# Attention and a gated MLP on one core: four buffers of converted weights, five of outputs, and copies on either engine

## The chip, the core and the metric

The kernel runs on one core of one Trainium2 chip. A core has five engines with queues of their own: PE (TensorE, matmuls), DVE (VectorE), ACT (ScalarE), POOL (GpSimd) and SP (SyncE, which here issues nearly all DMAs). Each executes its queue in order; semaphores tie them together. The metric is the device time of one execution in microseconds (us); less is better.

## What is computed

Attention over 8 batches, 12 heads, 448 positions and 64 channels, with normalised q and k, and then a gated MLP on its output:

```python
q_n, k_n = (rmsnorm(q, g_q), rmsnorm(k, g_k))
scores = scale * np.matmul(q_n, k_n.transpose(0, 1, 3, 2))
scores = scores - np.max(scores, axis=-1, keepdims=True)
attn = np.exp(scores)
attn = attn / (np.sum(attn, axis=-1, keepdims=True) + 1e-09)
x = np.matmul(attn, v)                      # (8, 448, 768) after the heads are joined
...
h = gelu(x @ w_in)                          # 768 -> 1024
u, v = h[..., :512], h[..., 512:]
v_n = (v - mu) / np.sqrt(var + 1e-06) * g_ln
v_s = np.einsum('ts,bsd->btd', w_sg, v_n) + b_sg[None, :, None]
out = x + (u * v_s) @ w_out
```

## The kernel before

**Precision.** Nearly every operand is held as two parts, a high and a low one of 16 bits (or two of fp32r for the last product), so that most products are three matmuls, and most conversions are a copy of the high part and a subtraction for the low one.

**Attention.** A unit is two pairs of heads; there are 24 units, three to a batch, and seven row tiles to a unit. For a row tile the PE writes scores `s` for two halves (12 matmuls of 64x448); the DVE takes the row minimum into `nm` (`jk`, 336 of them in all, 14 to a unit); ACT computes the exponential `ex` with its sums. `ex` is split into two 16-bit parts `ahl`, the high half on ACT, the low half on either engine; SP issues a DMA that transposes `ahl` into `at`. `ahl` lies in a ring of NAH = 3 buffers, so a new one waits until a transpose has left an old one. Then PE multiplies `at` by the parts of v (`vh`, `vl`) into `pv`, in two groups of row tiles a unit (four, then three), and spreads the reciprocal sums over partitions with the `row` matmuls. `row` is copied from PSUM by ACT, `sx` = `pv` times `row` is made by the DVE, and from it `xh` (ACT) and `xl` (POOL) are written to the output tile `x` of the unit. `x` lies in a ring of NX = 6: two batches.

**Preparation of a unit.** q and k are loaded (`qk`), squared (`sqk`), summed (`ss`) and scaled by POOL, split into `hl` and transposed by DMA into `qt`.

**Weights.** They arrive as 64-bit words, which the DVE decodes by integer operations: `dec` for w_in (12 chunks, `wi`), `wr` and `wo_l` for w_out (8 chunks). This is done while the first units run.

**MLP of a batch.** `mv` (the v half, 432 matmuls of 512 columns in all), a cluster of gelus on ACT between two loads of its function table, statistics and normalisation (`vg`, `vh`, `vl`), `mu` (the u half), a second cluster, `ms` (the product with w_sg), two operations and a split on the DVE and ACT (`gh`, `gl`), and `mo`, which adds the residual x and the product with w_out. `ot` copies `mo` from PSUM, and SP sends it out. `mo` reads the unit's `x`, so `x` stays occupied until the batch's MLP ends.

**What sets the order.** The code does not run operations in the order in which it is written. It records them on a tape (`Tape.record`), each with a running count as priority, lowered or raised by an offset: MOFF0 for the first batch's MLP, MOFF for the others', WOFF for the weights, GP for the gelu clusters. How many steps of each stream are recorded per pair of heads is set by SC, SV, WR and M0 to ML; WD is the pair at whose end the weights must all have been recorded, and CUTS says after which steps a group of `pv` may be interrupted. A planner (`Tape.schedule`) then plays a list schedule with costs of its own: an engine takes the ready task of the lowest count, PE prefers to stay in its present tile shape within HYST counts, and a copy that may run on two engines goes to the one that ends it earlier (`Tape.either`, `Tape.best`). The letters HI, EL, RW, OT, VH and so on name the engines allowed for a copy. The planner's order is what the engines execute; all operations are emitted by line 441.

Of the kernel before, what the change touches and what calls it, by code (L numbers as in the profile page):

```python
# [22 lines left out]
ASC = 2.0 ** 14  # L23


MOFF, MOFF0, GP = 300, 100, 350

HI, EL, LO, SQ, QH, QL, RW, XH, OT, GH, VH = "A", "VA", "V", "A", "AV", "G", "A", "A", "A", "A", "A"

UP, UNIT, DEN = 18.714973875118524, 2.0 ** -16, 2.0 ** -41  # L30

WR, M0, M1, MR, ML = 3, 8, 7, 11, 11

I0, WD = 5, 6

VC, UC, CP, MERGE = (2,3), (0,1,2), 'A', False

SC, SV = 7, 4

GRAM = False  # L40

# [1 line left out]

BANKS, MOST = 8, dict(pv=2, mm=4, mme=3, sc=6)
NQK, NVR, RAWB = 2, 2, 3
NAT, NAH, NQT, NVH, HLB, GV = 2, 3, 2, 4, 3, 3
NOT, NX, NEX = 2, 6, 2
DEC, XL, VL, WL = 'V', 'G', 'V', 'V'
RQ, OQ, SQ_, VQ, GLAT, KQ, XQ = 'S', 'S', 'S', 'S', (1100, 4000), 'S', 'S'
EXP_SET = "natural_log_exp_and_others"  # L50
BACC_KW = dict(dynamic_dma_scratch_size=1024)
TILE_KW = dict()

SWITCH, HYST = (133, 92), 160
BIAS = dict(A=0, V=0, G=0)
SLACK = (0, 0)
LONG = 500
WOFF = 0
CUTS = (5,14)
CA = 200  # L60
CV = 70
AG = 85
OVER, PATIENCE = dict(V=130, G=150), 300
START = dict(T=60, A=34, V=33, G=85, S=28, N=0)
AGAIN = dict(T=15, A=15, V=15, G=AG, S=15, N=15)

# [39 lines left out]
class Tape:  # L106
# [140 lines left out]
    def best(self, t, e, now, free, avail, port):  # L247

        mine = now + t.alts[e][1] + BIAS[e] + (max(0, port - now - OVER[e]) if t.alts[e][3] else 0)
        for f, (_, occ, _, _) in t.alts.items():  # L250
            if f != e:
                wait = sum(self.tasks[k].occ for p, k in avail[f] if p < t.prio and not self.tasks[k].alts)
                if max(free[f], now) + wait + occ + BIAS[f] < mine:
                    return False
# [194 lines left out]
def kernel(  # L449
# [256 lines left out]
    def load_qk(u, qs=None):  # L706
        if u >= NI // NG:
            return
        qs = qs or [LD[KQ if u else "S"]]
        b, h0 = u // NU, u % NU * 2 * NG  # L710
        qk = ld.tile([P, 2, 2, C7, D], F32, name="qk", bufs=NQK)
        for x, src in enumerate((q, k)):
            for j in range(NG):
                qs[x % len(qs)].dma_start(
                    out=qk[j * HP:(j + 1) * HP, x].rearrange("p h c d -> p h (c d)"),
                    in_=src[b, h0 + 2 * j:h0 + 2 * j + 2].rearrange("h (p c) d -> p h (c d)", c=C7))
        U[u] = dict(qk=qk)
# [161 lines left out]
    def pv(u, e):  # L879
# [12 lines left out]
        for k_, (j, (v_, o, hx)) in enumerate(steps):  # L892
            for h, (ks, c) in enumerate(hx):
                mm(out=pc[h * HP:(h + 1) * HP, j], lhsT=R[NG * u + j][v_][ks, c], rhs=av[ks, o + c, j, 0:n],
                   start=(k_ == 0), stop=(k_ == len(steps) - 1), skip_group_check=True)
            if k_ in CUTS:
                yield
# [222 lines left out]
    def low(gen, off):  # L1120

        def run():
            while True:
                tape.off = off
                tape.cut()
                try:
                    next(gen)
                except StopIteration:
                    return
                finally:  # L1130
                    tape.off = 0
                    tape.cut()
                yield
        return run()
# [6 lines left out]
    pend = None  # L1141
    wts = low(weights(), WOFF)
    load_qk(0, [SP, A] if EARLY else None)
# [116 lines left out]
```

## Time and profile before

| | us |
|---|---|
| median of three runs | 860.46 |
| lowest, highest | 859.57, 861.25 |
| span of the profiled execution | 856.1 |
| busy in it: PE | 739.2 (86%) |
| ACT | 715.0 (84%) |
| DVE | 664.1 (78%) |
| POOL | 364.9 (43%) |

The span goes from the first to the last instruction of one execution; the time of a run, 860.46 us in the median, also holds what lies around it. The shares of busy time are means over stretches with different limits, so the section with the rows cuts the span into four. All kernel operations carry line 441, so that they are told apart by the names of tiles.

### The profile page before, as it was taken

To read this page: it belongs to the slowest core of one execution; us is meant where nothing else is said; L and a number is where in the kernel's file an instruction comes from. 1 tells how busy PE (TensorE), PEld (TensorE's weight loads), DVE (VectorE), ACT (ScalarE), POOL (GpSimd) and SP (SyncE) were. 2 spreads that over 40 slices of the span, in tenths; PEclk is the share of its full clock that TensorE was granted. 3 is DMA by queue.
4 is the path that set the end of the run, shared out by engine and by line. 5 is a ranking of instruction groups with operands and counts; after the bars stand their busy time and mean duration, and the time that the engine had idled before them with its cause. 6 is when DMAs were issued, how large, how long until landed. Compare 5 with 4: busy or idle time off the path is not lost.

```text
span 856.1 us, 21095 instructions
## 1 busy us (share of the span) xinstructions
PE 739.2 (86%) x7766; PEld 471.9 (55%) x7766; DVE 664.1 (78%) x1658; ACT 715.0 (84%) x1480; POOL 364.9 (43%) x505
## 2 busy tenths in 40 slices
PE   0436768735899999999999999999999999999997
PEld 0223434423485568655855578556755586558557
DVE  6889998899967898878877888879877886484150
ACT  4687889997898999998988898899999998786451
POOL 2544442166635544463565356453463454111000
PEclk9667769986999999999999999999999999999999
DMA  6999999699999979999699989999999699637002
GB/s 172 242 256 211 214 216 177 158 205 210 196 238 214 212 154 192 222 216 198 148 201 234 208 165 225 223 184 180 207 216 211 149 204 184 124 73 156 19 1 74
DMA packets 433943, 155.97 MB, mean 182 GB/s; under 512 B 402544, under 2 KB 427696, under 8 KB 433840
## 3 DMA queue, kind: packets, MB, share of 16 engines
q1 hardware_dynamic: 433840, 154.63, 88.7%
q8 instruction: 61, 1.00, 0.5%
q14 instruction: 42, 0.34, 0.1%
HBM read 43.57 MB, written 11.01 MB: 64 GB/s over the span
## 4 chain that ended last, share of the span: by engine, by line
PE 42%; ACT 23%; DVE 16%; DMA 9%; issue 6%; SPq 2%; POOL 2%; ACTq 0%; DVEq 0%; POOLq 0%
PE pv L441 8%; DMA at<-ahl 6%; ACT ex L441 6%; PE s L441 5%; ACT ahl L441 5%; ACT L441 3%; DVE jk L441 3%; DVE dec L441 2%; DVE wr L441 2%; SPq L441 2%; ACT vg L441 1%; ACT u L441 1%; ACT sqk L441 1%; DVE vl L441 1%; DVE ahl L441 1%
## 5 line engine op out<-in xcount | busy, mean ns | idle before, releaser
L441 DVE TENSOR_SCALAR_CACHE_REDUCE jk<-s 128x448 bf16<-128x448 f32 x336 | 199.2, 615 | 36.9 <-PE s L441 36.4
L441 ACT ACTIVATE ex<-s,nm 128x448 int32<-128x448 f32 x336 | 212.4, 637 | 13.4 <-DVE jk L441 13.1
L441 ACT ACTIVATE ahl<-ex 128x896 f16<-128x896 uint16 x184 | 174.2, 953 | 9.0 <-DMA at<-ahl 8.3
L441 PE MATMUL s<-qt 64*64 64x448 f16 x2016 | 137.9, 375 | 48.6 <-DMA qt<-hl 21.7
L441 PE MATMUL pv<-at,vh 128*64 128x192 f16 (+3 forms) x1536 | 130.6, 271 | 28.1 <-DMA at<-ahl 24.9
L441 PEld LDWEIGHTS <-vh 128*64 128x64 f16 (+2 forms) x1792 | 101.4, 111 | 95.6 <-issue 56.8
L441 DVE TENSOR_SCALAR ahl<-ex 128x896 f16<-128x896 uint16 x152 | 113.6, 748 | 33.9 <-ACT ex L441 26.7
L441 PEld LDWEIGHTS <-qt 64*64 64x64 f16 x2016 | 63.0, 111 | 94.2 <-issue 53.4
L441 POOL TENSOR_TENSOR hl<-qk,hl 128x896 f16<-128x896 f32 (+2 forms) x69 | 93.7, 1364 | 32.7 <-DVE hl L441 8.2
L441 POOL TENSOR_TENSOR xl<-sx,xh 128x512 f16<-128x512 f32 (+1 forms) x48 | 50.5, 1052 | 102.4 <-ACT xh L441 58.8
L441 PEld LDWEIGHTS <-wi 128*128 128x128 f16 x576 | 54.7, 100 | 56.5 <-issue 9.9
L441 POOL TENSOR_TENSOR qk<-qk,ny 128x896 f32<-128x896 f32 x46 | 77.7, 1698 | 15.5 <-DVE ahl L441 6.6
L441 PEld LDWEIGHTS <-xh 128*128 128x128 f16 (+1 forms) x648 | 49.9, 102 | 46.2 <-issue 19.1
L441 PE MATMUL pv<-at,vl 128*64 128x192 f16 (+3 forms) x768 | 72.6, 269 | 0.0
L441 POOL TENSOR_TENSOR qk<-qk,gg 128x896 f32<-128x896 f32 x23 | 48.4, 2102 | 54.6 <-ACT sqk L441 32.6
L441 ACT ACTIVATION_READ_ACCUMULATOR ex<-s,nm 128x1 f32 x336 | 70.4, 210 | 0.0
L441 PEld LDWEIGHTS <-vl 128*64 128x64 f16 (+2 forms) x896 | 55.0, 111 | 15.4 <-DVE vl L441 2.8
L441 POOL TENSOR_SCALAR rx<-sums 128x8 f32<-128x8 f32 (+1 forms) x48 | 19.5, 406 | 98.7 <-ACT ex L441 96.8
L441 DVE TENSOR_REDUCE ss<-sqk 128x14 f32<-128x896 f32 x48 | 51.8, 1081 | 10.5 <-ACT sqk L441 10.4
L441 DVE TENSOR_TENSOR sx<-pv,row 128x512 f32<-128x512 f32 (+1 forms) x48 | 29.7, 619 | 28.4 <-PE pv L441 28.4
L441 ACT ACTIVATE sqk<-qk 128x896 f32<-128x896 f32 x48 | 45.8, 954 | 4.3 <-DMA qk<-in_q_dram 3.0
L441 PEld LDWEIGHTS <-xl 128*128 128x128 f16 (+1 forms) x408 | 36.7, 103 | 22.6 <-POOL xl L441 3.9
(1104 smaller groups left out, 1811.5 us busy)
## 6 DMA issues: line engine op xcount, KB each, us to landing
qk<-in_q_dram SPq DMA_DIRECT2D x48, 224.0 KB, 4.4
qk<-in_k_dram SPq DMA_DIRECT2D x48, 224.0 KB, 4.7
out_dram<-ot SPq DMA_DIRECT2D x56, 192.0 KB, 3.4
raw<-in_moe_w_in_dram SPq DMA_DIRECT2D x12, 512.0 KB, 5.1
vr<-in_v_dram SPq DMA_DIRECT2D x32, 192.0 KB, 3.8
vr<-in_v_dram SPq DMA_DIRECT2D x32, 144.0 KB, 3.9
rawo<-in_moe_w_out_dram SPq DMA_DIRECT2D x8, 384.0 KB, 3.9
at<-ahl SPq DMA_TRANSPOSE x168, 4.5
```

Source lines behind the costliest of these rows:

```text
L441: ins = getattr(q.nc_eng, op)(*first, *a, **kw)
```

## The change

It changes numbers and letters alone; every operation and its operands stay, and only engine, order and buffers differ.

- `ahl` gets four buffers (NAH), `x` five (NX). Both are 3584 bytes per partition.
- `row` (RW), `ot` (OT) and `vh` (VH, the normalised v of the MLP) may be copied by ACT or by the DVE instead of by ACT alone.
- MOFF0, GP, M1, ML, WOFF, WD, SV and CUTS move the recording of the MLP, the gelu clusters, the weights and `pv`.
- HYST, BIAS, OVER and PATIENCE alter the planner's choices.

```diff
--- before.py
+++ after.py
@@ -23,19 +23,19 @@
 ASC = 2.0 ** 14
 
 
-MOFF, MOFF0, GP = 300, 100, 350
-
-HI, EL, LO, SQ, QH, QL, RW, XH, OT, GH, VH = "A", "VA", "V", "A", "AV", "G", "A", "A", "A", "A", "A"
+MOFF, MOFF0, GP = 300, 60, 492
+
+HI, EL, LO, SQ, QH, QL, RW, XH, OT, GH, VH = "A", "VA", "V", "A", "AV", "G", "AV", "A", "VA", "A", "AV"
 
 UP, UNIT, DEN = 18.714973875118524, 2.0 ** -16, 2.0 ** -41
 
-WR, M0, M1, MR, ML = 3, 8, 7, 11, 11
-
-I0, WD = 5, 6
-
-VC, UC, CP, MERGE = (2,3), (0,1,2), 'A', False
-
-SC, SV = 7, 4
+WR, M0, M1, MR, ML = 3, 8, 10, 11, 12
+
+I0, WD = 5, 4
+
+VC, UC, CP, MERGE = (2, 3), (0, 1, 2), "A", False
+
+SC, SV = 7, 3
 
 GRAM = False
 
@@ -43,24 +43,24 @@
 
 BANKS, MOST = 8, dict(pv=2, mm=4, mme=3, sc=6)
 NQK, NVR, RAWB = 2, 2, 3
-NAT, NAH, NQT, NVH, HLB, GV = 2, 3, 2, 4, 3, 3
-NOT, NX, NEX = 2, 6, 2
-DEC, XL, VL, WL = 'V', 'G', 'V', 'V'
+NAT, NAH, NQT, NVH, HLB, GV = 2, 4, 2, 4, 3, 3
+NOT, NX, NEX = 2, 5, 2
+DEC, XL, VL, WL = 'V', "G", "V", 'V'
 RQ, OQ, SQ_, VQ, GLAT, KQ, XQ = 'S', 'S', 'S', 'S', (1100, 4000), 'S', 'S'
 EXP_SET = "natural_log_exp_and_others"
 BACC_KW = dict(dynamic_dma_scratch_size=1024)
 TILE_KW = dict()
 
-SWITCH, HYST = (133, 92), 160
-BIAS = dict(A=0, V=0, G=0)
+SWITCH, HYST = (133, 92), 137
+BIAS = dict(A=0, V=0, G=-200)
 SLACK = (0, 0)
 LONG = 500
-WOFF = 0
-CUTS = (5,14)
+WOFF = -22
+CUTS = (2, 19)
 CA = 200
 CV = 70
 AG = 85
-OVER, PATIENCE = dict(V=130, G=150), 300
+OVER, PATIENCE = dict(V=160, G=150), 351
 START = dict(T=60, A=34, V=33, G=85, S=28, N=0)
 AGAIN = dict(T=15, A=15, V=15, G=AG, S=15, N=15)
```

In the order that the planner makes, ACT gives away 31 of 56 `ot`, 26 of 48 `row` and 21 of 32 `vh`, and takes over 9 `ahl` and 7 `hl`; the DVE has the opposite. PE has the same 7747 matmuls.

The first place is the DVE while it decodes w_out, in the MLP of batch 0 (`wr` and `wo_l` are decoded weights, `jk` the row minima, `mv` and `st` the statistics of the layer norm, `ry` the reciprocal sums). Before:

```order
L441 TENSOR_TENSOR wo_l<-wr,wo_h 128x384
L441 TENSOR_SCALAR jk,nm<-s 128x448
L441 TENSOR_SCALAR wr<-rawo 128x384
L441 TENSOR_SCALAR jk,nm<-s 128x448
L441 TENSOR_SCALAR wr<-wr 128x384
L441 RECIPROCAL ry<-rx 128x6
L441 TENSOR_SCALAR jk,nm<-s 128x448 x2
L441 TENSOR_SCALAR wr<-wr 128x384
L441 TENSOR_SCALAR jk,nm<-s 128x448 x2
L441 SCALAR_TENSOR_TENSOR wr<-rawo,wr 128x384
```

After:

```order
L441 TENSOR_SCALAR wr<-rawo 128x384
L441 BN_AGGR mv<-st 128x2
L441 BN_STATS st<-vg 128x6
L441 TENSOR_SCALAR wr<-wr 128x384
L441 TENSOR_SCALAR wr<-rawo 128x384
L441 TENSOR_SCALAR wr<-wr 128x384 x2
L441 SCALAR_TENSOR_TENSOR wr<-rawo,wr 128x384
L441 TENSOR_SCALAR wr<-wr 128x384
L441 BN_AGGR mv<-st 128x2
```

Steps of the decoding stood singly between row minima; now they stand next to each other beside the statistics of the first layer norm, and the minima come later. The last `wo_l` has 370 instructions ahead of it before, 329 after; there are 78 minima among them before, 59 after.

The second place is ACT where the first output of unit 8 is written (`xh`; `ex` are exponentials, `ahl` converted weights, `sqk` squares, `vh` high parts of v). Before:

```order
L441 ACTIVATE nt_5046<-ss_4884,eps_90 128x28
L441 ACTIVATE ny_5062<-nt_5046 128x28
L441 ACTIVATE xh_5066<-sx_5044 128x4x2x64
L441 ACTIVATE row_5089<-row_5003 128x384
L441 ACTIVATE ex_5114,sums_4882<-s_5048,nm_5098 128x448
L441 ACTIVATE ot_4998<-mo__4947 128x384
L441 ACTIVATE ex_5114,sums_4882<-s_5051,nm_5098 128x448
```

After:

```order
L441 ACTIVATE vh_5160<-vr_4032,v_s_4993 128x448
L441 ACTIVATE xh_5187<-sx_4962 128x4x2x64
L441 ACTIVATE ex_5197,sums_4921<-s_5059,nm_5107 128x448
L441 ACTIVATE vh_5200<-vr_4679,v_s_4993 128x448
L441 ACTIVATE ex_5197,sums_4921<-s_5062,nm_5107 128x448
L441 ACTIVATE ex_5215,sums_4921<-s_5083,nm_5172 128x448
L441 ACTIVATE ahl_5227<-ex_5197 128x896
L441 ACTIVATE xh_5187<-sx_5218 128x3x2x64
L441 ACTIVATE ot_5239<-mo__5146 128x384
```

`xh` of this unit stood behind small steps of the norm, with a `row` copy and `ex` behind it; now it stands behind a copy of v, and exponentials and `ahl` of the next row tile follow it. With five buffers it waits for the last output matmul of batch 1 that reads the tile of unit 3, which on PE stands 195 instructions behind the end of this unit's `pv`; with six the tile of unit 2 was read 1720 instructions before that end.

## Rows read from the trace of the kernel before

**Rows 1.** The page: the span, and the shares of the chain by engine.

```profile
span 856.1 us, 21095 instructions
...
PE 42%; ACT 23%; DVE 16%; DMA 9%; issue 6%; SPq 2%; POOL 2%; ACTq 0%; DVEq 0%; POOLq 0%
```

**Rows 2.** Stretches: length; busy us of PE, PEld, DVE, ACT, POOL; clock, DMA share, GB/s.

```profile
0.00:119.30 119.30, 53.48 (x572) 30.32 (x573) 103.15 (x238) 83.70 (x165) 52.48 (x76) 0.74 1.02 220
119.30:234.90 115.60, 80.26 (x816) 44.67 (x813) 107.04 (x263) 103.56 (x210) 56.29 (x70) 0.86 0.91 190
234.90:780.30 545.40, 534.35 (x5850) 347.67 (x5850) 434.78 (x1115) 496.39 (x1052) 252.06 (x350) 1.00 0.95 190
780.30:856.10 75.80, 71.13 (x532) 49.28 (x530) 19.16 (x47) 31.37 (x56) 4.07 (x10) 0.99 0.22 52
```

**Rows 3.** Timeline of PE: start us, length us, instruction, xcount; two dense places.

```profile
310.53 1.33 PE L441 MATMUL s<-qt 64*64 64x448 f16 x24
311.79 0.44 PE L441 MATMUL pv<-at,vh 128*64 128x192 f16 x6
312.06 0.41 PE L441 MATMUL pv<-at,vl 128*64 128x192 f16 x6
...
272.42 0.59 PE L441 MATMUL mv__3870<-wi,xh 128*128 128x512 f16 x2
272.85 0.38 PE L441 MATMUL mv__3870<-wi,xl 128*128 128x512 f16 x1
```

**Rows 4.** Waits from 235 to 780 us: who waits, for whom, us in total, times, longest.

```profile
DVE ahl L441 <- DMA at<-ahl: 5.2, 6, 2.2
...
ACT ahl L441 <- DMA at<-ahl: 4.3, 6, 1.5
...
PE pv L441 <- DMA at<-ahl: 3.0, 4, 1.5
```

**Rows 5.** Timeline of DVE and PE near the first output matmul of batch 0.

```profile
225.94 0.61 DVE L441 TENSOR_TENSOR gl<-ms__2833,gh 128x448 fp32r<-128x448 f32 x1
...
235.45 0.61 DVE L441 TENSOR_TENSOR gl<-ms__2955,gh 128x448 fp32r<-128x448 f32 x1
...
231.75 0.22 PE L441 MATMUL mo__3068<-idn,xh 128*128 128x128 bf16 x1
```

**Rows 6.** Groups of DVE by form: xcount | busy us, mean ns of one | idle before.

```profile
L441 DVE TENSOR_SCALAR_CACHE_REDUCE jk<-s 128x448 bf16<-128x448 f32 x336 | 199.2, 615 | 36.9 <-PE s L441 36.4
...
L441 DVE DVE_READ_ACCUMULATOR jk<-s 128x1 f32 x336 | 27.5, 82 | 0.0
...
L441 DVE TENSOR_SCALAR ahl<-ex 128x896 f16<-128x896 uint16 x152 | 113.6, 748 | 33.9 <-ACT ex L441 26.7 <-DMA at<-ahl 7.0
...
L441 DVE TENSOR_REDUCE ss<-sqk 128x14 f32<-128x896 f32 x48 | 51.8, 1081 | 10.5 <-ACT sqk L441 10.4
...
L441 DVE CAST hl<-qk 128x896 f16<-128x896 f32 x13 | 12.1, 928 | 1.3 <-POOL qk L441 1.3
...
L441 DVE TENSOR_TENSOR qk<-qk,gg 128x896 f32<-128x896 f32 x1 | 1.1, 1091 | 0.0
...
L441 DVE RECIPROCAL ry<-rx 128x6 f32<-128x6 f32 x24 | 4.5, 187 | 0.9 <-POOL rx L441 0.4
...
L441 DVE TENSOR_TENSOR sx<-pv,row 128x512 f32<-128x512 f32 x24 | 16.5, 687 | 13.6 <-PE pv L441 13.6
...
L441 DVE CAST hl<-qk 128x512 f16<-128x512 f32 x11 | 4.8, 439 | 1.8 <-POOL qk L441 1.8
```

**Rows 7.** Groups of ACT by form, same columns.

```profile
L441 ACT ACTIVATE ahl<-ex 128x896 f16<-128x896 uint16 x184 | 174.2, 953 | 9.0 <-DMA at<-ahl 8.3
...
L441 ACT ACTIVATE row<-row 128x512 f32<-128x512 f32 x24 | 14.4, 602 | 6.0 <-PE row L441 5.9
...
L441 ACT ACTIVATE vh<-vg 128x512 f16<-128x512 f32 x24 | 13.8, 624 | 5.8 <-DVE vg L441 5.8
...
L441 ACT ACTIVATE ot<-mo__4865 128x384 f32<-128x384 f32 x1 | 0.5, 492 | 1.0 <-PE mo__4865 L441 1.0
```


## What was predicted

> **What bounds the kernel now.** I read the span first [rows 1], then the table of four stretches [rows 2], cut where the DVE has finished the 42nd, the 84th and the last of the 336 row minima (`jk`). In the third stretch, 545.4 us long, PE is busy for 534.35 us, or 98%, ACT for 496.39 (91%) and DVE for 434.78 (80%); the granted clock is 1.00, the 2.4 GHz level. In the first two the picture is turned round: between 119.3 and 234.9 us the DVE is busy for 107.04 of 115.60 us, and PE for 80.26. So the program has two halves. Up to about 235 us the DVE decodes the weights and everything queues behind it; afterwards the matmuls queue, almost without holes, until the end.
>
> A busy PE is a weak sign, because the records of pipelined matmuls overlap. So I look at where one starts after another [rows 3]. Twenty-four score matmuls (`s`) take from 310.53 to 311.79 us, 0.0525 us each; six `pv` of 192 columns take from 311.79 to 312.06, 0.045 each; two `mv` of 512 columns take from 272.42 to 272.85, 0.215 each. They follow each other without a pause. In the whole third stretch PE was seen to wait only about 11 us (545.40 less 534.35), of which the wait of `pv` for the transposed weights is 3.0 us [rows 4]. PE's queue is the path there.
>
> The Trainium skill, in "Perfetto Trace Analysis", section "Identifying the Most-Contended Engine", says not to trust matmul busy time, and to take occupancy for ACT and DVE and weight-load time for PE. By that rule ACT (91%) and not PE (weight loads 347.67 of 545.40 us, 64%) is the engine to relieve; what that would give is rival A. The starts one behind another speak against it, so I follow the starts.
>
> **The start of the output phase.** The instants that matter are those at which the first MLP's output matmuls (`mo`, batch 0) can run, since they fill a PE that has otherwise little to do. Before, the first stands at 231.75 us; the second and the fourth `gl` that they need left the DVE at 225.94 and 235.45 [rows 5]. The change records the decoding of the weights earlier (WOFF, WD) and the first MLP at a smaller offset (MOFF0). In the DVE's order the second `gl` is preceded by 388 instructions before the change and 366 after it. What is missing in front of it [rows 6]: 10 `jk` with the reading of their accumulator, 10 x (0.615 + 0.082) = 6.97; 6 `ahl`, 6 x 0.748 = 4.49; 2 `ss`, 2.16; two wide `hl` casts, 1.86; nine shorter ones from `ry` (0.187) to `qk` (1.091), together some 5.0. That is 20.5 us. What is new in front of it: 4 `row` copies and 3 `vh` casts. The trace has neither on the DVE; the nearest rows are `sx` (0.687, also from PSUM) and the `hl` cast of 512 (0.439), so 4 x 0.687 + 3 x 0.439 = 4.1 at most and about 3.6 with the narrow ones. Net: 16.9 us earlier. Up to the fourth `gl` it is 3 `jk`, 2 `ahl` and one `sx` more, 21.1 us. The DVE has hardly a hole there, so the time comes out in full. I take 16.9, since the second `gl` opens the gate, and put the first `mo` at 214.9 us; the other end is 21.1.
>
> This is not all gain, since the postponed attention work has to be made up. By counting the two orders up to the first `mo`, PE has by then issued 432 instead of 504 score matmuls, 384 instead of 480 `pv` (48 fewer of each width), and 128 instead of 156 `row`; the MLP's matmuls are the same 210. Priced from [rows 3]: 72 x 0.0525 = 3.8; 48 x 0.045 = 2.2; 48 wider `pv` at 4/3 of it, 2.9; 28 `row` at 2/3 of it, 0.8. Sum 9.7 us, which PE pays after the first `mo`. From there before needed 856.1 - 231.75 = 624.35 us; the change needs 624.35 + 9.7 = 634.0, and ends at 214.9 + 634.0 = 848.9. That is **-7.2 us**; with the fourth `gl` as gate, -11.4.
>
> **Changes of the matmuls' tile shape.** HYST, CUTS and SV regroup the matmuls on PE. Counted in the order, tile shape changes 365 times before and 351 after; behind the first `mo` it is 289 in both. The 14 saved lie where PE waits anyway. Zero, and at most 14 times some 0.1 us (an estimate from the step between `s` and its neighbours) either way.
>
> **Copies between ACT and DVE.** Counted in the orders, ACT gives the DVE 31 `ot` copies, 26 `row` copies and 21 `vh` casts, and takes back 9 `ahl` and 7 `hl` casts. On ACT that is 31 x 0.492 + 26 x 0.602 + 21 x 0.624 less 9 x 0.953 and less 7 at about the price of `vh` [rows 7], so 44 - 13 = 31 us off at most; on the DVE some 25 to 29 on top, priced as above. In the third stretch the DVE has 545.40 - 434.78 = 110 us free [rows 2], so the addition is covered there; if that cover were gone it would cost its 25 to 29. ACT's relief is worth nothing as long as PE's queue is the path; what is late next is PE itself.
>
> **Four `ahl` buffers.** ACT and DVE waited 4.3 and 5.2 us in the third stretch for a transposing DMA to release one of three buffers [rows 4]. These waits go, but ACT and DVE have slack there. Only the 3.0 us in which `pv` waited for the transposed weights touch PE. Bounds 0 and -3.0, and -11 if all of PE's waiting went; I take **-2.0**, because those waits follow late `ahl`.
>
> **Five `x` buffers.** The fifth-last unit's output must have been read by the last output matmul before a new unit may write. In PE's order the last reader stood 494 rows or more ahead of the end of the new `pv` before; now it stands behind it or close by at the units 8, 11, 14, 17 and 20. At unit 8 there are 113 matmuls between (47 `mo`, 41 `pv`, 24 `s`), priced at the starts above about 9.3 us; at 14 and 20 some 0.7 each, at 11 and 17 the reader comes 1.7 before the end, which is no wait. The `xh` copy stands on ACT with `ex`, `vh` and `ahl` of the next row tile behind it, and PE waits for these. While ACT waits, though, PE works through just those matmuls, so I take 0; the other end is 9.3 + 1.4 = 10.7, and 14 if units 11 and 17 paid theirs too.
>
> **The sum.** 856.1 - 7.2 - 2.0 = 846.9 us against the profiled span of 856.1 us. The median of the runs shown is 860.46, 4.4 above the span, for what lies around it; I carry that over: **851.2 us**.
>
> **Rivals.**
> A: ACT is the bound. For it: ACT busy 91%, ACT with 23% of the chain [rows 1]. Then nearly all of ACT's 31 us count, some 28 of them in the third stretch: 860.46 - 28 = 832. Against it: PE's holes are 11 us there, and no relief of ACT can give back more than those and the start's 7 to 11. It decides if PE's records hide waits. This is the case that the skill's rule above points to.
> B: the early start is eaten. At the first `mo` the change has 72 instead of 84 `jk` done; if ACT cannot make up the 12 missing halves of score work while the `mo` run, PE waits for `s` and the third stretch begins where it did. Time 860.46 + 0 to -1.5, about 860. For it: ACT's 91%; against: its relief.
> C, slower: the ring of five `x` buffers. If the wait of `xh` at unit 8 and its four smaller brethren comes out in full, PE starves after each, since `ex` of the next tile comes late. Price up to 14 us: 851.2 + 14 = 865. It decides against the change as soon as more than 9.2 of the 14 us are not covered.
> The Trainium skill's "TensorE: Matmul & The Clock Gate", section "Back-to-back issue gap", gives about 131 ns for a matmul of 512 columns in a sustained stream, by which the 432 such `mv` would be 432 x 0.084 = 36 us shorter (an estimate from that page's figure), PE would have slack and A's time would follow; the trace disagrees with 0.215 us a start [rows 3].
>
> **How the numbers follow.** Forecast 0.66 (851.2; its own range 846 to 856, from the gate at 21.1 us and from no gain by the buffers with a part of C's price); A 0.10; B 0.09; C 0.15. Faster by over 0.2% (1.7 us, about what a measurement of this kernel can tell from no change) are the forecast and A: 0.76; B is the same: 0.09; C is slower: 0.15. The range runs from 838, where half of A still lies (a start worth 11.4 with all of PE's 11 us of waiting gone), to 863, which takes in B and the lower half of C.
>
> **What the profile afterwards would show.** First `mo` of batch 0 near 215 us (212 to 220), DVE still over 90% busy up to there. Between that point and the end, about 634 us, PE over 97% busy, clock 1.00. ACT's busy time near 690 us and the DVE's near 688, with the end unmoved by that. No wait of `xh` above 2 us. The step on the start is wrong if the first `mo` comes after 225 us; the step on PE as the path is wrong if PE waits over 20 us in the third stretch, or if the end moves by much more than the first `mo` did.

## The result and the profile after

The changed kernel takes **838.5 us** (median of four runs, 837.55 to 841.94), against 860.02 us for the kernel before in the same series: ratio 0.9766, 95% interval 0.974 to 0.9792. That is 21.5 us less in the medians and 20 by the ratio; the prediction said 9.3 less (851.2). The direction and the range hold. The size doesn't, and the experiments show that the reason doesn't either.

The page of the changed kernel: span, busy time of the engines, and shares of the chain that ended last.

```profile
span 840.2 us, 21062 instructions
...
PE 733.8 (87%) x7766; PEld 471.7 (56%) x7766; DVE 685.0 (82%) x1719; ACT 693.0 (82%) x1418; POOL 365.1 (43%) x506
...
PE 55%; DVE 18%; ACT 10%; DMA 7%; issue 6%; SPq 2%; POOL 2%; DVEq 0%; ACTq 0%; POOLq 0%
```

The execution profiled here was the slowest of the four (841.94 us); in each of the four the time is 1.74 to 1.83 us above the span. In the chain PE has risen and ACT has fallen to 10% [rows 1]. ACT's and the DVE's busy times (693.0 and 685.0) are near the 690 and 688 of the forecast.

The four stretches, cut again at the 42nd, the 84th and the last row minimum (columns: from and to, length, busy us and instructions of PE, PEld (PE's weight loads), DVE, ACT and POOL, granted clock, DMA share, GB/s):

```profile
0.00:118.90 118.90, 51.29 (x572) 29.42 (x573) 103.57 (x241) 84.33 (x164) 47.81 (x69) 0.77 1.04 220
118.90:233.60 114.70, 89.95 (x894) 56.79 (x894) 101.97 (x259) 103.08 (x209) 58.84 (x74) 0.88 0.95 192
233.60:768.60 535.00, 525.64 (x5809) 339.60 (x5808) 459.74 (x1176) 478.08 (x1003) 254.40 (x354) 1.00 1.01 196
768.60:840.20 71.60, 66.92 (x494) 45.89 (x493) 19.75 (x49) 27.51 (x46) 4.07 (x10) 0.99 0.17 43
```

Beside [rows 2], the 84th minimum comes only 1.3 us earlier (233.6 for 234.9), but PE has been busy for 7.5 us more by then (51.29 and 89.95 in the first two stretches, for 53.48 and 80.26). The third stretch is 10.4 us shorter, the last 4.2. PE looks as full as before: 98% in both third stretches.

The gate of the output phase, on the timeline of DVE and PE:

```profile
207.39 0.61 DVE L441 TENSOR_TENSOR gl<-ms__2510,gh 128x448 fp32r<-128x448 f32 x1
208.59 0.61 DVE L441 TENSOR_TENSOR gl<-ms__2524,gh 128x448 fp32r<-128x448 f32 x1
...
208.18 0.22 PE L441 MATMUL mo__2700<-idn,xh 128*128 128x128 bf16 x1 [0.80 <-DVE gtl L441]
```

The second `gl` moved from 225.94 [rows 5] to 208.59, 17.35 us for a forecast of 16.9 (both are the times at which it starts). The first `mo` moved by 23.6 us, and it starts before the second `gl` does: it waited 0.80 us for the `gtl` behind the first `gl`.

What is left of waits in the third stretch (engine, what waited, for whom; us in all, times, longest):

```profile
PE s L441 <- ACT ex L441: 1.7, 1, 1.7
PE pv L441 <- ACT ex L441: 1.1, 1, 1.1
...
PE pv L441 <- DMA at<-ahl: 0.9, 2, 0.8
```

```profile
ACT ex L441 <- DVE jk L441: 15.0, 15, 3.5
...
ACT xh L441 <- DVE sx L441: 10.1, 16, 1.3
```

The waits of `ahl` for a free buffer, 5.2 and 4.3 us in [rows 4], are gone, and `pv` waits 0.9 us instead of 3.0 for the transposed weights. ACT has got the longer wait, 15.0 us for the DVE's row minima; in the kernel before it is 7.5.

### The profile page after: what moved, and what is told of

The parts are those of the page before. It is cut to its first block, busy times and chain, and to the rows that moved or that the text cites. A ratio compares the mean times of both kernels' runs of the same rounds, so it can differ in the third digit from the quotient of the medians.

```text
span 840.2 us, 21062 instructions
## 1 busy us (share of the span) xinstructions
PE 733.8 (87%) x7766; PEld 471.7 (56%) x7766; DVE 685.0 (82%) x1719; ACT 693.0 (82%) x1418; POOL 365.1 (43%) x506
## 4 chain that ended last, share of the span: by engine, by line
PE 55%; DVE 18%; ACT 10%; DMA 7%; issue 6%; SPq 2%; POOL 2%; DVEq 0%; ACTq 0%; POOLq 0%
PE pv L441 10%; PE s L441 8%; DMA at<-ahl 4%; DVE jk L441 3%; ACT ex L441 3%; SPq L441 2%; DVE ahl L441 2%; ACT ahl L441 2%; PE row L441 2%; DVE vl L441 2%; DVE dec L441 1%; DVE sx L441 1%; DMA qk<-in_k_dram 1%; DVE wr L441 1%; DVE ss L441 1%
## 5 line engine op out<-in xcount | busy, mean ns | idle before, releaser
L441 PE MATMUL s<-qt 64*64 64x448 f16 x2016 | 144.5, 373 | 53.9 <-ACT ex L441 23.2
L441 ACT ACTIVATE ahl<-ex 128x896 f16<-128x896 uint16 x193 | 180.3, 949 | 3.9 <-DMA at<-ahl 3.0
L441 PEld LDWEIGHTS <-vh 128*64 128x64 f16 (+2 forms) x1792 | 106.4, 113 | 83.5 <-issue 37.8
L441 DVE TENSOR_SCALAR ahl<-ex 128x896 f16<-128x896 uint16 x143 | 109.1, 765 | 17.3 <-ACT ex L441 16.0
L441 PEld LDWEIGHTS <-qt 64*64 64x64 f16 x2016 | 65.0, 110 | 96.4 <-issue 56.7
L441 POOL TENSOR_TENSOR hl<-qk,hl 128x384 f16<-128x384 f32 (+2 forms) x69 | 95.1, 1388 | 31.9 <-DVE hl L441 6.6
L441 PE MATMUL pv<-at,vl 128*64 128x192 f16 (+3 forms) x768 | 82.8, 275 | 6.3 <-DVE vl L441 6.3
L441 PEld LDWEIGHTS <-vl 128*64 128x64 f16 (+2 forms) x896 | 56.8, 113 | 36.4 <-issue 11.5
L441 ACT ACTIVATE xh<-sx 128x512 f16<-128x512 f32 (+1 forms) x48 | 27.6, 576 | 30.8 <-DVE sx L441 30.6
```

What stands on the lines that cost most here:

```text
L441: ins = getattr(q.nc_eng, op)(*first, *a, **kw)
```

## The experiments

Times are given by each kernel's ratio to the kernel before on the same chip; a difference in us between two kernels is the difference of their ratios times 859 us, about the median of before in these series. By the intervals given with the ratios, such a difference is good to some 3 us either way. There are two kinds of kernels: those for which the planner made a new order, and those in which the order of one of the two originals is held word for word and only one thing is exchanged. The second kind is the cleaner one, since a new order differs everywhere.

### Parts of the change, each with a new order

`b_start`: the kernel before with the start numbers alone.

```diff
-MOFF, MOFF0, GP = 300, 100, 350
+MOFF, MOFF0, GP = 300, 60, 350
-I0, WD = 5, 6
+I0, WD = 5, 4
-WOFF = 0
+WOFF = -22
```

> The kernel before with MOFF0 60, WOFF -22 and WD 4 alone. Theory 1 (the end is set by the PE work still to be done when the DVE has finished its 84th row minimum): counted in its order, PE has issued 100.9 us of matmul work by then (before 90.0, after the change 104.6) and the DVE comes there 2 us later, so -9.6 us against the kernel before: about 850. Theory 2 (ACT is the bound and its relief made the gain): ACT's work is the same, so 860, no change. Theory 3 (the three start numbers make the whole gain): about 838.

859.55 us, ratio 1.0008 (0.999 to 1.0026): nothing. Yet the first `mo` stands 10.6 us earlier than at 231.75 [rows 5]:

```profile
221.19 0.23 PE L441 MATMUL mo__2951<-idn,xh 128*128 128x128 bf16 x1
```

Counted in its order and priced by starts (0.052 us for an `s`, 0.044 and 0.058 for `pv`, 0.174, 0.19 and 0.216 for 384, 448 and 512 columns), PE has only 1.7 us more work left at its first `mo` than the kernel before at its own. By the prediction's way of summing, 8.9 us had to come out at the end. None did: from the first `mo` to the end it takes 635.5 us (856.7 - 221.19), where the kernel before takes 624.35.

`b_plan`: the kernel before with the planner's remaining numbers alone.

```diff
-SWITCH, HYST = (133, 92), 160
+SWITCH, HYST = (133, 92), 137
-BIAS = dict(A=0, V=0, G=0)
+BIAS = dict(A=0, V=0, G=-200)
-CUTS = (5,14)
+CUTS = (2, 19)
-OVER, PATIENCE = dict(V=130, G=150), 300
+OVER, PATIENCE = dict(V=160, G=150), 351
...
```

(GP 492, M1 10, ML 12 and SV 3 too.)

> The kernel before with the planner's numbers alone (HYST, BIAS, OVER, PATIENCE, CUTS, GP, M1, ML, SV), its copies, buffers and start offsets kept. Theory 1: by its order PE has issued 106.5 us of work at the 84th minimum, the DVE comes there 2 us later than before, so -15.6: about 844.5. Theory 2 (ACT): 860. Theory 3 (start numbers): 860.

868.92 us, 1.0105 (1.0081 to 1.0129): 9 us slower.

`b_copies` and `b_startcopies`: the copies on either engine, without and with the start numbers.

```diff
-HI, EL, LO, SQ, QH, QL, RW, XH, OT, GH, VH = "A", "VA", "V", "A", "AV", "G", "A", "A", "A", "A", "A"
+HI, EL, LO, SQ, QH, QL, RW, XH, OT, GH, VH = "A", "VA", "V", "A", "AV", "G", "AV", "A", "VA", "A", "AV"
```

> The kernel before with row, ot and vh copies allowed on the DVE too, and nothing else. Theory 4 (two queues of nearly equal length after the 84th minimum, PE's and ACT's; the later sets the end): ACT gets 19 us shorter, PE's lead at the 84th minimum grows by 4.4 us only, so PE is left as the limit: some 5 us faster, about 854. Theory 2 (ACT alone): 17 us faster or more, as the changed kernel lost 17 when the copies went back, about 842.

> The kernel before with the three start numbers and the copies. Theory 4: PE's lead is 9.8 us and the DVE comes 2.6 us later, and ACT no longer holds it back: 7 to 10 us faster, 850. Theory 2 (ACT alone): as b_copies, whatever that is. If start and copies were all of the change: 838.5.

855.07 us, 0.9953 (0.9934 to 0.9972), and 854.86 us, 0.9949 (0.9931 to 0.9968): 4 us for the copies, nothing more for the start beside them.

`b_startbufcop`: start numbers, copies and the buffers (`NAH` 4, `NX` 5) together; only the planner's remaining numbers are those of before.

> The kernel before with the start numbers (two offsets and the distance), the buffers (four of the converted weights, five of the outputs) and the copies on either engine, but with the planner's remaining numbers as they were. Theory: the three together relieve TensorE's start, ScalarE and the ring of converted weights at once, and the remaining numbers alone were worth nothing (they made the kernel before slower): 836 to 843 us, the changed kernel's time. Rival, the remaining numbers are needed in this company: 848 to 856 us, near the kernel with start numbers and copies (854.9).

853.47 us, 0.9934 (0.9909 to 0.9959). The theory that these three relieve three limits at once and make up the change, falls: the remaining numbers, which cost 9 us in the kernel before, are worth 14 in this company.

From the other side, the changed kernel with one part undone: `a_nostart` (MOFF0 100, WD 6, WOFF 0), `a_nobufs` (NAH 3, NX 6), `a_nocopies` (the letters of before).

> The changed kernel with MOFF0, WOFF and WD of before. Theory 4: PE has 106.5 us done at the 84th minimum, but the DVE comes there 7.6 us later than in the changed kernel: 838.5 + 7.6 - 2.0 = 844. Theory 2 (ACT alone): 838.5, no loss, since ACT's work is the same.

> The changed kernel with three ahl and six x buffers as before. Theory 4: the DVE comes to the 84th minimum 5 us later with the same PE work done, and the waits for the transposing DMA return: 838.5 + 5 + 0 to 2 = 843.5 to 845.5. Theory 2: ACT has 6 us more work, 843. If the buffers do nothing: 838.5.

> The changed kernel with row, ot and vh copies on ACT alone again, planned anew. Theory 1: PE has issued 106.1 us of work at the 84th minimum and the DVE comes there 1.6 us earlier than in the changed kernel, so 836 to 840, no loss against the changed kernel (838.5). Theory 2 (ACT is the bound): some 25 to 31 us of ACT work come back, about 865.

851.7 us, 0.9918 (0.9888 to 0.9949); 856.7 us, 0.9965 (0.9947 to 0.9984); 855.35 us, 0.9949 (0.9929 to 0.9968). Each undone part costs 13 to 17 us of 21, so they don't add up: each seems to be worth nearly the whole. But of nine replanned kernels, the changed one too, eight lie between 851 and 869. That says that the gain sits in one order, and not that a part owns it.

### One thing exchanged, the order held

`a_frozen`: the changed kernel's order on every queue, with each `row`, `ot` and `vh` copy that it gives to the DVE put back on ACT at the same place.

```diff
         for t in self.schedule():
+            if "A" in t.alts and t.eng == "V" and t.alts["A"][0][0][3]["out"].tensor.name.split(".")[0] in ("row", "ot", "vh"):
+                t.eng = "A"
+                t.calls, t.occ, t.lat, t.port = t.alts["A"]
             for c in t.calls:
```

> The changed kernel in its own order, instruction for instruction, but each row, ot and vh copy that the planner gave to the DVE is issued on ACT at the same place. Theory 1 (PE's queue is the path): 838.5 within 3 us. Theory 2 (ACT is the bound): 41 us of copies return to ACT, which has some 57 us free in the steady stretch; 855 to 868.

855.91 us, 0.996 (0.9941 to 0.9979): 17 us slower than the changed kernel, although PE's order is the same and the first `mo` comes only 1.4 us later. Its first `mo`, and its third stretch:

```profile
209.58 0.22 PE L444 MATMUL mo__2700<-idn,xh 128*128 128x128 bf16 x1 [0.82 <-DVE gtl L444]
```

```profile
235.00:783.20 548.20, 528.74 (x5809) 340.21 (x5809) 437.80 (x1107) 504.80 (x1070) 254.96 (x354) 1.00 0.99 191
```

The stretch is 13 us longer; ACT has 26.7 us more (504.80 for 478.08), the DVE 21.9 less.

Is that ACT's load? `a_act`, `a_dve` and `a_pe` add work to one engine of the changed kernel, in its own order: 84 small copies into a tile that nothing reads, behind every third `ex` or `jk`, or 96 of the `mu` products issued twice, so that those sums hold them twice.

```diff
                 ins = getattr(q.nc_eng, op)(*first, *a, **kw)
+                if op == "activation" and c[3]["out"].tensor.name.startswith("ex"):
+                    self.extra += 1
+                    if 84 <= self.extra < 336 and self.extra % 3 == 0:
+                        tc.nc.scalar.activation(out=self.scratch, in_=self.swapt, func=AF.Copy)
```

> The changed kernel in its own order, with ScalarE given 84 more copies of 128 x 128 f32 into a scratch tile that nothing reads, one behind every third exponential between the 84th and the 336th: about 20 us of ScalarE. Its busy time in the stretch would go from 478 to 498 us. Theory of near-equal limits: ScalarE has about 11 us of room (its share is 0.894, and kernels that it seems to bind stand at 0.91 to 0.92), the rest costs 1.09 us each: the time rises by 6 to 13 us. Rival, TensorE's queue alone is the path, as the prediction had it: 0 to 2 us. Rival, ScalarE binds the changed kernel's stretch already: 20 to 22 us.

840.01 us, 0.9779 (0.975 to 0.9809).

```diff
+                if op == "tensor_scalar" and c[3]["out"].tensor.name.startswith("jk"):
...
+                        tc.nc.vector.tensor_copy(out=self.scratch, in_=self.swapt)
```

> The changed kernel in its own order, with VectorE given 84 more copies of 128 x 128 f32 into a scratch tile that nothing reads, one behind every third minimum between the 84th and the 336th: about 17 us of VectorE, from 460 to 477 us of a stretch of 535 us. Theory of near-equal limits: VectorE is not among the limits (its share 0.859 would be 0.89), the time rises by 0 to 5 us. Rival, the copies that came to VectorE have made it the next bound, since the waits of ScalarE for VectorE's minimum are the longest left (15 us): 10 to 18 us.

850.44 us, 0.9902 (0.9875 to 0.993).

```diff
+                if op == "matmul" and c[3]["out"].tensor.name.startswith("mu_") and not c[3]["start"] and not c[3]["stop"]:
+                    self.extra += 1
+                    if 64 <= self.extra < 448 and self.extra % 4 == 0:
+                        getattr(q.nc_eng, op)(*a, **kw)
```

> The changed kernel in its own order, with TensorE given 96 more matmuls in the stretch between the 84th and the 336th minimum: every fourth of the middle products of the hidden layer (mu) is issued twice, so those sums hold some products twice. By start-to-start times of the trace that is about 18 us of TensorE's queue. Theory of near-equal limits: the changed kernel's stretch is bound by TensorE's work (its length is 1.07 times that work), so the time rises by 16 to 21 us. Rival, ScalarE binds the changed kernel's stretch: TensorE has no room (98% busy) but would take ScalarE's place only for what lies above it, so the rise is 5 us or less. Rival, the engines hold each other up in their order and none binds: each of the three additions costs about half of its length, 9 us here.

854.58 us, 0.9955 (0.9936 to 0.9974). Their third stretches, from the 84th to the last minimum, of `a_act`, `a_dve` and `a_pe`, one fence each:

```profile
233.10:769.10 536.00, 527.38 (x5809) 339.84 (x5808) 460.96 (x1174) 492.87 (x1086) 254.44 (x354) 1.00 0.99 195
```

```profile
234.10:779.40 545.30, 531.23 (x5810) 340.75 (x5809) 481.06 (x1258) 479.58 (x1003) 252.67 (x354) 0.99 0.99 192
```

```profile
230.50:780.30 549.80, 542.55 (x5904) 348.79 (x5903) 455.37 (x1174) 479.85 (x1003) 252.59 (x354) 1.00 0.99 190
```

ACT took 14.8 us more (492.87 for 478.08) for 1.1 us of time: it has room for that much, and the theory that ACT binds the changed kernel falls. The DVE took 21.3 us more for 11.7 us, PE 96 matmuls (some 18 us at 0.19) for 16.2 us. So ACT's load, up to some 15 us of it, does not explain the 17 us of `a_frozen`; an addition as large as its 26.7 us was not run. The other reading is the place: a copy that stands between two chains of matmuls and comes late in ACT's queue. Two kernels tell these apart: as `a_frozen`, but only the 31 `ot` go back (`a_fr_ot`), or only the 21 `vh` (`a_fr_vh`); the edit is that of `a_frozen` with one name.

> The changed kernel in its own order; of the copies that it gives to VectorE only the 31 output copies (ot) go back to ScalarE. Place theory (what counts is a copy that stands between two chains of TensorE's work): no matmul reads these, they only free a bank and feed a DMA; ScalarE has room (15 us of added copies cost 1.5 us) and VectorE has none (21 us of added copies cost 12 us): -5 to +2 us against the changed kernel (838.5). Load theory: a third of the 17 us that all three kinds of copies cost, 5 to 6 us slower.

841.34 us, 0.9803 (0.9788 to 0.9817): 3.2 us, a little above the place theory's bound, below the load theory's; with some 3 us either way this run alone does not tell the two apart.

> The changed kernel in its own order; only the 21 high halves of the gated values (vh) that it gives to VectorE go back to ScalarE, where one takes 0.62 us (0.42 on VectorE), and VectorE's low half waits for it across the engines. Place theory: 5 to 10 us slower than the changed kernel, with waits of TensorE for ScalarE's vh. Load theory: a third of the 17 us, 5 to 6 us.

849.19 us, 0.9889 (0.9871 to 0.9907): 10.6 us, at the top of the place theory's 5 to 10 and above the load theory's, for less ACT time than the `ot` took (21 x 0.62 = 13.0 us against 31 x 0.49 = 15.2). With `ot` and `a_act` beside it, the amount of ACT's work does not explain this; the place does. Its waits in the third stretch:

```profile
DVE vl L444 <- ACT vh L444: 14.4, 12, 4.8
...
PEld L444 <- ACT vh L444: 5.3, 4, 2.6
...
PE ms__7753 L444 <- ACT vh L444: 2.2, 1, 2.2
...
PE ms__12731 L444 <- ACT vh L444: 1.4, 1, 1.4
```

And the same waits in the changed kernel:

```profile
DVE vl L441 <- ACT vh L441: 1.9, 3, 0.9
...
PEld L441 <- DVE vh L441: 1.1, 2, 0.7
...
PE ms__4374 L441 <- DVE vh L441: 0.3, 1, 0.3
```

`vh` is made from `vg`, `vl` from both, and the `ms` matmuls need them. With `vh` on the DVE, `vg`, `vh` and `vl` follow each other on one queue, a `vh` takes 0.42 instead of 0.62 us, and of the waits across engines little is left (1.9 us, where 11 of the 32 `vh` stay on ACT). With `vh` on ACT, it stands behind whatever ACT has in its queue, the DVE waits for it 14.4 us, and PE with its weight loads behind that. One such place, first in the changed kernel, where the DVE makes the `vh`, then in `a_fr_vh`:

```profile
474.86 0.28 DVE L441 CAST vh<-vg 128x256 f16<-128x256 f32 x1
477.50 0.35 PE L441 MATMUL ms__7753<-ws_h,vh 128*128 128x448 f16 x1
```

```profile
474.45 1.28 ACT L444 ACT_TABLE_LOAD   x1
...
478.06 1.28 ACT L444 ACT_TABLE_LOAD   x1
479.36 0.42 ACT L444 ACTIVATE vh<-vg 128x256 f16<-128x256 f32 x1
...
479.83 0.36 PE L444 MATMUL ms__7753<-ws_h,vh 128*128 128x448 f16 x1 [2.16 <-ACT vh L444]
```

On ACT the `vh` stands behind a whole cluster of gelus with its two table loads, and PE, which has the same order in both kernels, waits. Followed matmul by matmul, PE falls 2.4 us further behind the changed kernel at this point and 1.8 at `ms__12731`, which waits for a `vh` behind another such cluster: 4.2 of the 6.9 us by which the two profiled executions differ (847.1 and 840.2). How much the longer copy and the way across engines add to the standing in the queue was not separated.

Now the prediction's prices in the order that it looked at. `b_ring4` and `b_frcop` hold the order of the kernel before: one gets four buffers of `ahl` and five of `x`, the other the same 78 copies on the DVE that the changed kernel has there.

```diff
                 shape, dtype = tl.args
+                if tl.kw["name"] == "ahl":
+                    tl.kw["bufs"] = 4
+                if tl.pool.name == "xp":
+                    tl.kw["bufs"] = 5
```

> The kernel before in its own order on every engine, with four buffers of converted weights and five units of x, which is the change's fourth buffer alone. The prediction's price of the two: -2.0 us (bounds 0 and -3), so 857. Rival, the fourth buffer is worth as much as in the changed kernel, whose version without it and replanned was 18 us slower: 842 to 848. Rival, the fifth x unit for the sixth holds the start up: above 860.

861.17 us, 1.0035 (1.0008 to 1.0061): 3 us slower, not 2 faster. The trace tells the two buffers apart. The waits of `ahl` for a free buffer are gone, but `pv` still waits for the transposed weights (3.0 us before [rows 4]):

```profile
PE pv L445 <- DMA at<-ahl: 3.1, 4, 1.4
```

And with five `x` buffers an `xh` copy, which stands at 245.84 us without a wait in the kernel before, waits for an output matmul (`mo`), and PE waits for ACT after it:

```profile
250.50 0.63 ACT L445 ACTIVATE xh<-sx 128x512 f16<-128x512 f32 x1 [3.66 <-PE mo__3402 L445]
...
259.01 0.76 PE L445 MATMUL s<-qt 64*64 64x448 f16 x10 [1.79 <-ACT ot L445]
```

Followed matmul by matmul in the same order, PE is 1.0 us behind the kernel before ahead of this place and 4.4 behind it afterwards; at the end it is 2.9.

```diff
         for t in self.schedule():
+            if hasattr(t, "to_v"):
+                t.eng = "V"
+                t.calls, t.occ, t.lat, t.port = t.to_v
             for c in t.calls:
```

> The kernel before in its own order, with those row, output and v copies moved from ScalarE to VectorE at their places that the changed kernel has on VectorE (26, 31 and 21, by their number in the program). The prediction's price: 0 us, 858 to 860. Rival, the copies are worth their 17 us in this order too: 841 to 844. Between (place theory: what a shorter wait of TensorE gives back in this order too, less what VectorE's own queue loses): 849 to 856, near the replanned kernel with the copies (855).

868.58 us, 1.0119 (1.0104 to 1.0134): 10 us slower. The very same copies that are worth 17 us in the one order cost 10 in the other. ACT's third stretch is 24 us lighter for it, the DVE's as much heavier:

```profile
238.50:790.70 552.20, 537.81 (x5850) 348.14 (x5850) 459.04 (x1185) 472.42 (x985) 248.73 (x350) 1.00 0.95 188
```

Last, the first step of the prediction itself, in before's order: `b_lesspe` leaves out 96 of the middle `mu` products, `b_act` adds the 84 small copies to ACT.

```diff
+                if op == "matmul" and c[3]["out"].tensor.name.startswith("mu_") and not c[3]["start"] and not c[3]["stop"]:
+                    self.extra += 1
+                    if 64 <= self.extra < 448 and self.extra % 4 == 0:
+                        continue
                 ins = getattr(q.nc_eng, op)(*first, *a, **kw)
```

> The kernel before in its own order, with 96 of the middle products of the hidden layer (mu) left out in the stretch between the 84th and the 336th minimum, every fourth, so those sums lack some products: about 18 us less of TensorE's queue. The prediction's first step (TensorE's queue is the path of the kernel before): 16 to 20 us faster, 839 to 843. Rival, a second limit lies close behind (ScalarE at 0.91, or the order of its queue): 3 to 8 us faster. Rival, TensorE's work is not the path at all, as the start numbers alone suggested: 0 to 2 us.

858.51 us, 0.9999 (0.998 to 1.0017).

> The kernel before in its own order, with ScalarE given 84 more copies of 128 x 128 f32 into a scratch tile that nothing reads, one behind every third exponential between the 84th and the 336th (15 us of ScalarE by the changed kernel with the same addition, where they cost 1.5 us). TensorE's queue alone is the path: 0 to 3 us slower than before. Rival, ScalarE is a limit beside it in the kernel before: 8 to 16 us slower.

862.14 us, 1.0032 (1.0017 to 1.0048). The third stretches of `b_lesspe` and of `b_act`:

```profile
235.60:781.40 545.80, 521.99 (x5755) 339.19 (x5755) 434.66 (x1115) 496.55 (x1052) 252.10 (x350) 0.99 0.94 191
```

```profile
236.10:785.90 549.80, 535.85 (x5850) 347.68 (x5850) 437.86 (x1117) 509.95 (x1136) 252.10 (x350) 1.00 0.97 189
```

With 95 matmuls fewer in the stretch by the records, that of the kernel before is as long as ever, 545.8 us for 545.4 [rows 2]. One thing besides the work differs: in two places of `b_lesspe` the granted clock falls, where it is 1.00 in the kernel before.

```profile
480.00:490.00 10.00, 7.56 (x51) 3.47 (x49) 8.44 (x21) 9.74 (x18) 4.59 (x6) 0.84 1.10 232
570.00:580.00 10.00, 8.18 (x103) 4.45 (x103) 7.58 (x19) 8.43 (x21) 6.19 (x16) 0.83 0.87 174
```

By these rows that is at most 3.3 us of PE's time (10 x 0.16 + 10 x 0.17, an estimate) of the 18 taken out. PE, 98% busy, was not what set the stretch's length, at least not through these products. Nor was ACT's load: 13.6 us more cost 2.8.

## Why the prediction was wrong

**The first step failed: "PE's queue is the path there".** It was concluded from a PE busy for 98% of the third stretch, from starts without pauses and from some 11 us of seen waits [rows 2 to 4]. `b_lesspe` refutes it. The starts in [rows 3] are true, but they are a few bursts; work priced by such starts fills 510 of the 545 us (the matmuls counted in the order, at the prices under `b_start`). Of the other 35 the records show 11 as idle; the rest would have to lie in small pauses under records whose ends are modelled, which was not shown by itself. With some 18 us of matmuls gone, PE's busy time fell by only 12.4 us (534.35 to 521.99) and the end did not move.

**The start.** The part on the DVE was right: 17.35 us measured for 16.9 worked out. The gate was not. Before, PE came to its first `mo` from its own queue, without a wait, 5.2 us after the second `gl` had ended (226.55). In the changed kernel the first `mo`, which reads `x` and no `gl`, starts at 208.18, ahead of the second `gl` at 208.59; what it waited for ends with the `gtl` of the first. So the `mo` moved by 23.6 us, 6.7 more than the step had. (225.94 and 235.45, at which the prediction lets the two `gl` leave the DVE, are the times at which they start.) The work postponed by that, 9.7 us in the prediction, is 9.4 by the count at the two first `mo` (588.8 us left, before 579.4). From the first `mo` to the end the profiled execution took 632.0 us (840.2 - 208.18); the prediction said 848.9 - 214.9 = 634.0, and 2.0 less for the buffers. So the sum came out, and the gap between the forecast's span of 846.9 and the measured 840.2 is as large as these 6.7 us. But that is luck: the step holds only if PE's time behind the first `mo` grows by no more than the work put off, and by itself an earlier start does not do that. Beyond the work priced by starts, PE's way from the first `mo` to the end holds 45.0 us in the kernel before (624.35 - 579.4) and 43.2 in the changed one (632.0 - 588.8), but 54.4 in `b_start` (635.5 - 581.1) and 56.5 in `a_frozen` (854.9 - 209.58 - 588.8). `b_start` has an earlier first `mo` and no earlier end, which is the time that rival B named, in the kernel before; `a_frozen` has the changed kernel's start and 17 us less of its gain.

**Copies "worth nothing as long as PE's queue is the path".** The condition was false, and so was the price of 0 in both orders: +10 us in the order of before, -17 in the new one. So was the cover that the prediction saw in the DVE's 110 free us: in `b_frcop` the DVE's third stretch has 24.3 us more (459.04 for 434.78), and the time rises although ACT's falls. New order and copies go together: against the kernel before, the new order with these copies on ACT (`a_frozen`) is worth 3 us, the copies in the old order cost 10, both together are worth 20. What gives the gain of the copies in the new order is not the amount by which ACT is relieved, as rival A had it. For `vh` it was shown (10.6 of the 17 us) that a short step between two chains of matmuls no longer stands in ACT's queue. `ot` has about 3; what is left for `row` was not run by itself. Why the copies cost 10 us in the old order was not found.

**Four `ahl` buffers, -2.0.** In before's order the waits of `ahl` did vanish, but `pv`'s 3.0 us stayed 3.1: they did not follow late `ahl`, as the step had it (0.9 us is left of them in the changed kernel, whose order differs everywhere). What the fourth buffer is worth in the changed kernel's order was not run. **The ring of `x`** was rightly put at no visible cost in the changed kernel: the longest wait of `xh` in the third stretch is 1.3 us, and longer ones, up to 6.7, stand only in the last stretch and end with `sx`, as in the kernel before (up to 7.3). Rival C did not come there. In before's order its mechanism did: `b_ring4` lost 3.4 us of PE's time behind one wait of `xh`, so that matmuls which PE still has do not always cover it.

**The time around the span.** The prediction carried over 4.4 us between span and median. Only some 1.75 us lie outside the span; the rest was the distance of that one execution from the median. By bookkeeping, of the 12.7 us by which 851.2 missed, this is 2.6, the first `mo` 6.7, and the last 3.4 the distance of the changed kernel's profiled execution (841.94) from its median.

**Rival A and the skill's rule.** 832 lies nearer than 851.2, but its mechanism isn't what was found. The Trainium skill, "Perfetto Trace Analysis", section "Identifying the Most-Contended Engine", has one find the engine to relieve by occupancy and weight-load time, which here is ACT; the run disagrees that ACT's amount of work sets the end, since 13.6 us more of it cost 2.8. Neither fullness of PE nor that of ACT said what would count.

**The signs that the prediction named did not catch this.** From the first `mo` to the end PE is busy for 617.68 of 632.02 us (97.7%, forecast over 97%), and ACT's and the DVE's busy times came near the forecast. Two signs of the start missed: the first `mo` at 208.18 lies outside 212 to 220, and up to it the DVE is busy for 185.18 us (89%, forecast over 90%). But none that was to say that a step is wrong came: PE waits 9.4 us in the third stretch (535.00 - 525.64), not over 20, and the end did not move by more than the first `mo`. They were signs of the changed kernel, while the false step was about the kernel before.

**What stays open.** Which chain sets the third stretch of the kernel before was not found; as far as `b_lesspe` and `b_act` go, it is neither PE's nor ACT's amount of work; of PE's matmuls only `mu` products were left out, not `s` or `pv`. The part of the DVE and of the transposing DMAs there was not tried by taking work from them, and the DMA engines are a rival that no run touches: their busy share in the third stretch is 0.95 before and 1.01 in the changed kernel. For the changed kernel, work added to PE comes out almost whole (16.2 of 18) and to the DVE by half (11.7 of 21.3); that work taken away would come back was not shown. And why the remaining planner's numbers cost 9 us alone and are worth 14 beside the rest is only known as a result.

## What to carry to other kernels

An engine that is 98% busy, with starts one behind another, isn't yet the path: leave some of its work out, in the order as it is, and see whether the end moves, before prices are hung on it. Where a planner makes the order, price an edit with the order held; edits that are worth nothing or less alone (start, buffers, planner's numbers) were worth 13 to 17 us each in company here, so parts cannot be summed. Of copies that may go to either engine, look first at the ones between two chains of matmuls and at what they stand behind in the queue: here 21 `vh` were worth 10.6 us and 31 `ot` about 3, in one order.

## What had not been expected of the hardware

That PE's busy time in the records does not follow its work one for one: 96 matmuls fewer in the same 545 us, about 18 us at their start distance, took 12.4 us off it, and 98% became 95.6% with no change of the end. Up to 3.3 us of the difference can be the two places where the granted clock fell to 0.84 and 0.83; the rest was not explained.
